# Scaling the low words of float64 weights on GpSimd instead of ScalarE in an attention and gating kernel

## The chip, the cores and the metric

The kernel runs on one core of a Trainium2 chip. The core has five engines with queues of their own: TensorE (PE, matrix products and transposes into PSUM), VectorE (DVE), ScalarE (ACT), GpSimd (POOL) and SyncE (SP, which here issues most of the DMA transfers). Each takes its own queue in order, and an instruction starts when its engine has come to it and the semaphores it waits for are set. The metric is the device time of one execution in microseconds (us), as the median of several runs. PEld is the loading of weights into PE, which overlaps the products.

## The reference

Attention with a bias from running sums, then two gated mixing layers. B = 4 batches, H = 8 heads, S = 576 positions, D = 64.

```python
scores = scale * np.matmul(q, k.transpose(0, 1, 3, 2))
cum = np.cumsum(np.maximum(s, 0.0), axis=-1)
bias = -(cum[:, :, :, None] - cum[:, :, None, :])
scores = np.where(causal, -1000000000.0, scores + np.minimum(bias, 0.0))
attn = np.exp(scores - np.max(scores, axis=-1, keepdims=True))
attn = attn / (np.sum(attn, axis=-1, keepdims=True) + 1e-09)
x = np.matmul(attn, v)                    # heads side by side: (B, S, 512)
...
gate = 1.0 / (1.0 + np.exp(-gate_pre))    # gate_pre: 5-tap causal convolution of x with conv_w
x = gate * (x @ w_val) @ w_out
...
h = np.maximum(x @ w_in, 0.0)
u, v = h[..., :512], h[..., 512:]
v_n = (v - mean(v)) / np.sqrt(var(v) + 1e-06)
v_s = np.einsum('ts,bsd->btd', w_spatial, v_n) + b_spatial[None, :, None]
out = (u * v_s) @ w_out
```

The inputs q, k, v and s arrive as float32. The scale factors that build the dense weights are float64 numbers, so the weights w_val, conv_w, w_out (of both layers) and w_in arrive as float64, and the kernel turns them into float32 itself, then splits each into a high and a low part for products of more than one pass.

## The kernel before

The program runs over 32 heads (8 per batch). For one head, `scores` lets PE form score tiles in PSUM (L222, from head 8 on L224 and L225), DVE adds the mask and takes the row's extreme (L233, tiles p and nm), and ACT takes the exponential (L238). `transposes` turns p on PE (L279) and ACT copies the result to pt (L281). After every second head, `pv` multiplies by v (L303) and DVE scales with the reciprocal sums R into x (L306 to L309). R takes a way of its own: DVE forms the reciprocals rin (L248), PE transposes them (psr, L253), ACT copies them (rt, L255) and issues a store to r_d (L256), and SP loads them back, spread over the partitions (R, L262). `conv` then forms z from x on ACT (L318) and DVE (L321).

Between the heads, `more` draws background work from a queue of Python generators. For the first 16 heads this is the preparation of the weights. `first_steps` starts with conv_w, then prepares w_out and w_val chunk by chunk, then the first half of w_in, and folds w_out into w_in on PE (`fold`, L420 to L422). `second_steps` and `third_steps` do the rest, beside the first batch's mixing (`mixing_a`, `mixing_b`). From the second batch on, the mixing of a batch runs between the heads of the next one. The sigmoid of z runs on ACT (L514, for the last batch L517); between exponentials and sigmoids ACT loads another function table.

Each chunk of float64 weights goes through `from_f64`. SP loads 128 x 512 pairs of 32-bit words into r (tile wg for the early chunks with k below 3, else wr). `up` and `low` are every second word of r. ACT takes the absolute value of the upper words (L382, into a), DVE clamps it (L383), masks the sign (L384) and shifts and joins (L385); ACT scales the lower words by 2^-29 with a rounding to int32 (L388), and POOL adds both parts as integers (L389). Then `fold_prep` or `weight_prep` takes the high part on ACT (L73, `hi_of`) and the low part on DVE (L80, `lo_of`). There are 21 such conversions, 20 of full size and the small one of conv_w. The first 13 are held behind the last score reading on DVE (`paced`). POOL has little else to do: the low parts of gated values (g and y) and of v, and two small steps of the normalisation (L557, L559).

The order in each engine's queue is not the order of the code. The program is built with a scheduler that simulates the queues and puts the instructions of all engines into an order by priority and its own estimates of durations.

Of the kernel before, what the change touches and what calls it, by code (L numbers as in the profile page):

```python
# [10 lines left out]
U32 = mybir.dt.uint32  # L11
AF = mybir.ActivationFunctionType
ALU = mybir.AluOpType
# [11 lines left out]
def tile_stickbreak_attention_moe(  # L25
# [39 lines left out]
    V, G, A, T, SY = nc.vector, nc.gpsimd, nc.scalar, nc.tensor, nc.sync  # L65

    def f(ap):
        return ap.bitcast(F32)
# [65 lines left out]
    def tmp(name, dt=F32):  # L134
        return mid.tile([128, S], dt, tag="tmp", name=name, bufs=2)
# [230 lines left out]
    def from_f64(src, n):  # L366

        k = count[0] % 5
        count[0] += 1
        if count[0] <= 13 and k < 3:  # L370
            if k == 0 and "g" not in W:
                W["g"] = mid.tile([128, NP * (2 * S + 64)], I32, tag="g", name="wg")
            r = W["g"][:, k * 1536:k * 1536 + 1024]
            a = f(W["g"][:, k * 1536 + 1024:k * 1536 + 1536])
        else:
            r = mid.tile([128, 1024], I32, tag="wr", name="wr", bufs=2)
            a = tmp("wa")
        W["r"] = r
        r, a = r.rearrange("p (c t) -> p c t", t=2)[:, 0:n, :], a[:, 0:n]
        SY.dma_start(r, src.rearrange("p (c t) -> p c t", t=2))  # L380
        up, low = r[:, :, 1], r[:, :, 0]
        A.activation(a, f(up), AF.Abs, scale=65536.0)  # L382
        V.tensor_scalar(out=a, in0=a, scalar1=F64_HIGH, scalar2=F64_LOW, op0=ALU.min, op1=ALU.max)  # L383
        V.tensor_scalar(out=up, in0=up, scalar1=-2 ** 31, scalar2=None, op0=ALU.bitwise_and)  # L384
        V.scalar_tensor_tensor(out=up, in0=a.bitcast(I32), scalar=3, in1=up, op0=ALU.logical_shift_left,  # L385
                               op1=ALU.bitwise_or)

        A.activation(low, low.bitcast(U32), AF.Copy, scale=2.0 ** -29)  # L388
        G.tensor_tensor(out=a.bitcast(I32), in0=low, in1=up, op=ALU.add)  # L389
        return a  # L390

    @paced
    def fold_prep(kc, j):

        if j is None:
            wh, wl, src = wo_h, wo_l, woT[:, kc * 1024:(kc + 1) * 1024]
        else:
            if j not in wi:
                wi[j] = [wtmp.tile([128, NP, 512], F32R, tag=f"wi{x}", name=f"wi{x}") for x in "hl"]
            wh, wl = wi[j]  # L400
            src = w_in[:, kc, j * 1024:(j + 1) * 1024]
        t = from_f64(src, 512)
        hi_of(A, wh[:, kc, :], t)
        lo_of(V, wl[:, kc, :], t, wh[:, kc, :])

    @paced
    def weight_prep(src, dst, mc):
        t = from_f64(src[mc], 512)
        w = W["r"].rearrange("p (t c) -> p t c", t=2).bitcast(F32R)
        hi_of(A, w[:, 0, :], t)  # L410
        lo_of(V, w[:, 1, :], t, w[:, 0, :])
        SY.dma_start(dst[mc], f(w))
# [218 lines left out]
    def first_steps():  # L631
        nonlocal cw
        cw = early.tile([128, NP, 5], F32, name="cw")
        V.tensor_copy(cw, from_f64(conv_w, 20).rearrange("p (c k) -> p c k", k=5))
        order = [(lambda mc=mc: weight_prep(w_val, wv_d, mc)) for mc in KC]
        order += [(lambda mc=mc: fold_prep(mc, None)) for mc in KC]
        order = order[4:] + order[:4]
        for o in order:
            o()
            yield  # L640
        for kc in KC:
            fold_prep(kc, 1)
            yield
        for ec in range(4):
            fold(ec, 1)
            yield 2.56
# [140 lines left out]
```

## Time and profile before

| | us |
|---|---|
| median of 3 runs | 516.34 (516.25 to 516.61) |
| the profiled execution | 515.71 |
| its span | 513.9 |
| PE, DVE, ACT, POOL busy | 481.8, 315.6, 338.5, 128.3 |
| mean granted clock of PE | 0.987 |

The rows come from one profiled execution. A row names the source line, the engine, the operation, the tiles written and read (numbers of buffers left out), the shape, and then durations; "<-" behind an idle time names what ended it. Times of a stretch are counted from the span's start.

### The profile page before, as it was taken

The page shows a single profiled execution, that of the slowest core. Times are in us where ns is not written, and L with a number is a line of the kernel's source. Part 1 is how long each engine was busy: PE and PEld are TensorE (multiplying, and loading weights), DVE is VectorE, ACT ScalarE, POOL GpSimd, SP SyncE. Part 2 cuts the span into 40 slices and gives each one's busy share as a digit, 9 for nine tenths or more (in the row PEclk, how much of TensorE's full clock was granted, in tenths as well). Part 3 has the DMA queues.
Part 4 walks back from the last instruction along what each step waited for, and adds up shares of the span by engine and source line. Part 5 has one row for each costly group of instructions (what it writes and reads, how often), then busy time and mean ns, then how long its engine had stood idle before and what let it go on. Part 6 is the DMA issues. An engine that isn't in the chain of part 4 may idle for free.

```text
span 513.9 us, 9133 instructions
## 1 busy us (share of the span) xinstructions
PE 481.8 (94%) x3138; PEld 402.4 (78%) x3138; DVE 315.6 (61%) x835; ACT 338.5 (66%) x819; POOL 128.3 (25%) x162
## 2 busy tenths in 40 slices
PE   8697978879999999998999999899998999999997
PEld 5454545767778887986969897888878889998997
DVE  5588988878978984843579476544767435125120
ACT  2999797697787965893748666785889724225322
POOL 5121112017360104101235023002243013146140
PEclk9798989999999999999999999999999999999999
DMA  3964897346752644276640413675611071700002
GB/s 92 253 206 145 263 331 191 110 112 214 238 197 82 185 145 124 74 215 198 179 119 13 131 39 87 186 221 169 177 28 34 5 248 45 237 2 1 0 8 86
DMA packets 51855, 69.28 MB, mean 135 GB/s; under 512 B 23968, under 2 KB 39488, under 8 KB 51808
## 3 DMA queue, kind: packets, MB, share of 16 engines
q1 hardware_dynamic: 46880, 63.88, 42.2%
q10 hardware_dynamic: 4928, 4.80, 2.8%
q8 instruction: 25, 0.41, 0.3%
q14 instruction: 22, 0.18, 0.1%
HBM read 55.96 MB, written 9.16 MB: 127 GB/s over the span
## 4 chain that ended last, share of the span: by engine, by line
PE 49%; ACT 3%; DMA 3%; issue 1%; DVE 1%; ACTq 0%; DVEq 0%
PE psm L420 9%; PE psm L421 9%; PE psm L422 9%; PE pso L303 5%; PE pst L279 4%; PE psm L592 3%; PE psm L594 2%; PE psm L593 2%; PE pss L224 2%; DMA out<-ot 2%; PE pss L225 2%; DMA wv<-wv_d 1%; ACT L238 1%; PE psm L595 1%; PE psm L596 1%
## 5 line engine op out<-in xcount | busy, mean ns | idle before, releaser
L238 ACT ACTIVATE p<-p,nm 64x64 f32<-64x64 f32 (+4 forms) x160 | 88.4, 554 | 10.7 <-DVE nm L233 10.3
L281 ACT ACTIVATE pt<-pst 128x512 f32<-128x512 f32 (+2 forms) x128 | 60.2, 498 | 30.0 <-PE pst L279 24.3
L233 DVE CUSTOM_DVE_ANT_0 p<-pss,mask 64x64 f32<-64x64 f32 (+4 forms) x160 | 63.0, 413 | 19.3 <-PE pss L225 8.5
L279 PE MATMUL pst<-ident,p 128*128 128x128 f32 x416 | 64.3, 281 | 3.2 <-ACT p L238 3.2
L80 POOL TENSOR_TENSOR g<-gt,g 128x288 fp32r<-128x288 f32 x32 | 29.3, 918 | 125.5 <-ACT g L73 100.1
L279 PEld LDWEIGHTS pst<-ident,p 128*128 128x128 f32 x416 | 51.2, 145 | 10.9 <-ACT p L238 4.5
L321 DVE SCALAR_TENSOR_TENSOR z<-x,cw,z 128x575 f32<-128x575 f32 (+1 forms) x64 | 55.2, 863 | 7.1 <-ACT z L318 6.6
L80 POOL TENSOR_TENSOR y<-gt,y 128x288 fp32r<-128x288 f32 x32 | 27.8, 872 | 111.2 <-ACT y L73 111.2
L303 PE MATMUL pso<-pt,vraw 128*64 128x512 f32 (+4 forms) x320 | 54.0, 446 | 0.1
L224 PE MATMUL pss<-qk 128*64 128x64 f32 (+1 forms) x144 | 43.6, 321 | 1.8 <-ACT pt L281 1.2
L225 PE MATMUL pss<-kd,cn 66*64 66x64 f32 (+1 forms) x144 | 41.4, 295 | 0.0
L222 PE MATMUL pss<-raw 128*128 128x320 f32 (+4 forms) x96 | 32.2, 448 | 8.6 <-DVE nm L233 5.3
L420 PE MATMUL psm<-g,wch 128*128 128x288 f32 x128 | 38.4, 304 | 1.3 <-ACT v L544 1.3
L497 DVE TENSOR_TENSOR gt<-psm,z 128x288 f32<-128x288 f32 x32 | 14.5, 454 | 40.7 <-PE psm L422 33.0
L303 PEld LDWEIGHTS pso<-pt,vraw 128*64 128x64 f32 (+1 forms) x320 | 19.5, 137 | 25.3 <-issue 17.6
L592 PE MATMUL psm<-wsh,vh 128*128 128x288 f32 x128 | 38.3, 303 | 0.4 <-DVE gt L497 0.4
L593 PE MATMUL psm<-wsh,vl 128*128 128x288 f32 x128 | 37.6, 298 | 0.0
L422 PE MATMUL psm<-g,wch 128*128 128x288 f32 x128 | 37.5, 297 | 0.0
L594 PE MATMUL psm<-wsl,vh 128*128 128x288 f32 x128 | 37.5, 296 | 0.0
L421 PE MATMUL psm<-g,wcl 128*128 128x288 f32 x128 | 37.4, 295 | 0.0
L497 DVE TENSOR_TENSOR gt<-psm,u 128x288 f32<-128x288 f32 x32 | 14.5, 454 | 35.1 <-PE psm L596 26.5
L420 PE MATMUL psm<-y,wv 128*128 128x288 f32 x96 | 29.2, 305 | 3.8 <-ACT ot L607 3.7
(168 smaller groups left out, 1327.0 us busy)
## 6 DMA issues: line engine op xcount, KB each, us to landing
raw<-in_qk SPq DMA_DIRECT2D x24, 448.0 KB
wv<-wv_d SPq DMA_DIRECT2D x12, 512.0 KB
wv<-wo_d SPq DMA_DIRECT2D x12, 512.0 KB
R<-r_d SPq DMA_DIRECT2D x32, 160.0 KB
out<-ot ACTq DMA_DIRECT2D x32, 144.0 KB
vraw<-in_vp SPq DMA_DIRECT2D x32, 128.0 KB
cn<-qk SPq DMA_DIRECT2D x24, 144.0 KB
raw<-in_qk SPq DMA_DIRECT2D x48, 64.0 KB
```

What stands on the lines that cost most here:

```text
L80: eng.tensor_tensor(out=out_, in0=in_, in1=f(hi), op=ALU.subtract)
L224: T.matmul(pst[0:m, o:o + b - a], qa[:, q0:q0 + m], kb[:, k0 + a:k0 + b], start=True, stop=False)
L233: LAST["V"] = V.tensor_tensor_reduce(out=row[:, a:b], in0=src, in1=mask[0:m, o:o + b - a], scale=-0.125, scalar=3.0e38 if a == 0 else nm[0 ...
L238: A.activation(row, row, AF.Exp, bias=nm[0:m, i:i + 1], scale=-1.0, accum_out=sm[h // 2 % 2][0:m, h % 2, i:i + 1])
L279: T.transpose(pt[:, 128 * t:128 * t + 128], p[:, o:o + 128], ident[:, way:way + 128])
L281: A.activation(PT[h][:, to:to + n], pt[:, o:o + n], AF.Copy)
L303: m = T.matmul(to[64 * j:64 * j + 64], vs[j][k0:, 4 + (c == 4) if c > 3 else c, :], pts[j][k0:, o:o + to.shape[1]], start=c in (0, 5), sto ...
L321: V.scalar_tensor_tensor(out=z[:, d:], in0=x[:, :S - d], scalar=cw[:, p, k:k + 1], in1=z[:, d:], op0=ALU.mult, op1=ALU.add)
L420: T.matmul(pt, ah, bh, start=j == 0, stop=False)
L421: T.matmul(pt, al, bh, start=False, stop=False)
L422: T.matmul(pt, ah, bl, start=False, stop=j == n - 1)
L592: T.matmul(o, vh[c][:, cs], wsh[:, c, hs[hf]], start=c == 0, stop=False)
```

## The change

One line of `from_f64` changes. The scaling of the lower words, with the rounding to int32, is issued to POOL as a multiplication by a scalar instead of to ACT as a copy with a scale. The add that follows was on POOL before and stays there.

```diff
@@ -385,7 +385,7 @@
         V.scalar_tensor_tensor(out=up, in0=a.bitcast(I32), scalar=3, in1=up, op0=ALU.logical_shift_left,
                                op1=ALU.bitwise_or)
 
-        A.activation(low, low.bitcast(U32), AF.Copy, scale=2.0 ** -29)
+        G.tensor_scalar(out=low, in0=low.bitcast(U32), scalar1=2.0 ** -29, scalar2=None, op0=ALU.mult)
         G.tensor_tensor(out=a.bitcast(I32), in0=low, in1=up, op=ALU.add)
         return a
```

Since the scheduler lays out all queues anew, the order differs on every engine from the second head on. Each engine has the same instructions as before, but for the 21 that move from ACT to POOL and two more table loads on ACT.

The first place is POOL's queue during the conversions of w_out (in the early heads); wg_183 is the shared tile of the early chunks, wr and wa with a number are the words and the result of one later chunk, and + marks what is new at this place.

```order
+L388 TENSOR_SCALAR wr_260<-wr_260 128x512
+L389 TENSOR_TENSOR wg_183<-wg_183 128x512
+L388 TENSOR_SCALAR wr_322<-wr_322 128x512
+L389 TENSOR_TENSOR wa_261<-wr_260 128x512
+L388 TENSOR_SCALAR wg_183<-wg_183 128x512 x2
+L389 TENSOR_TENSOR wa_323<-wr_322 128x512
```

Where adds (L389) stood one behind the other before, the scaling of the next chunk now stands between them, ahead of the add of the chunk before it.

The second place is DVE's queue around x1, the x of the second pair of heads. nm_744 belongs to head 7 and nm_575 to head 5; the rows without an input read out a sum. Before:

```order
L233 ISA p1_128,nm_744<-pss_762,mask_99 128x320
L233 ISA nm_744 128x1
L385 SCALAR_TENSOR_TENSOR wg_183<-wg_183 128x512
L233 ISA p1_128,nm_744<-pss_788,mask_99 128x448
L233 ISA nm_744 128x1
L306 TENSOR_TENSOR x1_552<-pso_553,R_523 128x384
L308 TENSOR_TENSOR x1_552<-pso_553,R_523 128x128
L309 TENSOR_TENSOR x1_552<-psq_554,R_523 128x64
L80 TENSOR_TENSOR wil_604<-wa_606,wih_603 128x512
```

and in the changed kernel:

```order
L233 ISA p1_128,nm_575<-pss_593,mask_99 128x320
L233 ISA nm_575 128x1
L383 TENSOR_SCALAR wa_606<-wa_606 128x512
L384 TENSOR_SCALAR wr_605<-wr_605 128x512
L306 TENSOR_TENSOR x1_552<-pso_553,R_523 128x384
L308 TENSOR_TENSOR x1_552<-pso_553,R_523 128x128
L309 TENSOR_TENSOR x1_552<-psq_554,R_523 128x64
L233 ISA p1_128,nm_575<-pss_616,mask_99 128x448
```

x1 has moved up by two heads. Its reciprocal, rin_468, stood 53 rows ahead of it and now stands 26 rows ahead. On PE, the products of the same pair (L303) stood behind the first score tiles of head 6 and now stand ahead of those of head 5.

The third place is ACT's queue at the last head: z_4084 is the gate of the last batch, L580 a copy of the mixing. Before:

```order
L238 ACTIVATE p1_128,sm1_122<-p1_128,nm_4699 128x576
L580 ACTIVATE u_4610<-psm_4769 128x288
L281 ACTIVATE pt_4709<-pst_4738 128x512
L281 ACTIVATE pt_4709<-pst_4763 128x512
L580 ACTIVATE u_4610<-psm_4796 128x288
L517 ACT_TABLE_LOAD
L517 ACTIVATE z_4084<-z_4084 128x576
```

and in the changed kernel:

```order
L580 ACTIVATE u_4610<-psm_4744 128x288
L517 ACT_TABLE_LOAD
L517 ACTIVATE z_4084<-z_4084 128x576
L238 ACT_TABLE_LOAD
L238 ACTIVATE p1_128,sm1_122<-p1_128,nm_4699 128x576
L580 ACTIVATE u_4610<-psm_4769 128x288
L580 ACTIVATE u_4610<-psm_4796 128x288
```

The third sigmoid of the last batch has moved ahead of the last exponential, which takes one more table load here, and one more before the fourth sigmoid.

## Rows read from the trace of the kernel before

**Rows 1.** The page: busy time, share and instructions by engine; granted clock in 40 slices.

```profile
PE 481.8 (94%) x3138; PEld 402.4 (78%) x3138; DVE 315.6 (61%) x835; ACT 338.5 (66%) x819; POOL 128.3 (25%) x162
...
PEclk9798989999999999999999999999999999999999
```

**Rows 2.** Busy time by stretch: length, then PE, PEld, DVE, ACT, POOL; clock, DMA.

```profile
10.00:28.00 18.00, 13.90 (x56) 9.20 (x55) 10.12 (x44) 14.18 (x42) 2.29 (x3) 0.81 0.90 252
28.00:82.00 54.00, 46.03 (x240) 27.58 (x239) 49.05 (x129) 47.76 (x120) 12.10 (x10) 0.94 0.74 228
82.00:110.00 28.00, 21.50 (x124) 15.76 (x122) 22.92 (x63) 21.28 (x44) 1.27 (x1) 1.00 0.43 109
110.00:190.00 80.00, 79.63 (x514) 65.98 (x515) 67.13 (x161) 63.27 (x158) 27.49 (x29) 1.00 0.59 184
190.00:513.90 323.90, 312.49 (x2188) 277.89 (x2186) 160.26 (x424) 189.51 (x454) 78.09 (x98) 1.00 0.36 104
```

**Rows 3.** Waits in 28 to 82 us (R: 10 to 110): total, times, longest.

```profile
PE pss L222 <- DVE nm L233: 5.3, 9, 1.4
PE psr L253 <- DVE x L309: 1.4, 1, 1.4
PE pss L224 <- ACT pt L281: 1.2, 1, 1.2
...
DVE p L233 <- PE pst L279: 2.2, 3, 1.3
DVE p L233 <- PE pss L222: 1.3, 3, 0.8
...
ACT wr L73 <- POOL wa L389: 2.2, 1, 2.2
...
DVE x L306 <- DMA R<-r_d: 4.5, 3, 1.6
```

**Rows 4.** L388 in 28 to 82 us (ns min/median/max); two ACT rows, in order of time.

```profile
L388 ACT ACTIVATE wg<-wg x6: 662/680/706, 32.2 to 72.3; 128x512 int32<-128x512 uint32 x6
L388 ACT ACTIVATE wr<-wr x5: 662/694/717, 29.8 to 79.1; 128x512 int32<-128x512 uint32 x5
...
16.26 0.68 ACT L388 ACTIVATE wg<-wg 128x512 int32<-128x512 uint32 x1
16.82 0.45 ACT L238 ACTIVATE p<-p,nm 128x192 f32<-128x192 f32 x1
```

**Rows 5.** In order of time: start us, us; then line L384 on DVE.

```profile
34.59 1.10 POOL L389 TENSOR_TENSOR wa<-wr 128x512 int32<-128x512 int32 x1 [2.87 <-ACT wo_h L73]
34.71 1.27 DVE L384 TENSOR_SCALAR wg<-wg 128x512 int32<-128x512 int32 x1
...
79.76 1.48 DVE L80 TENSOR_TENSOR kd<-raw,qk 64x576 fp32r<-64x576 f32 x1
...
L384 DVE TENSOR_SCALAR wg<-wg x9: 169/415/1274, 13.6 to 77.3; 128x512 int32<-128x512 int32 x8, 128x20 int32<-128x20 int32 x1
```

**Rows 6.** POOL operations by line: ns min/median/max, first and last start.

```profile
L104 POOL TENSOR_SCALAR_AFFINE_SELECT ident<-ident x2: 241/268/295, 6.2 to 6.4; 128x128 f32<-128x128 f32 x1, 128x64 f32<-128x64 f32 x1
...
L389 POOL TENSOR_TENSOR wa<-wr x12: 1038/1072/1367, 30.4 to 174.4; 128x512 int32<-128x512 int32 x12
...
L80 POOL TENSOR_TENSOR vl<-v,vh x16: 1277/1296/1721, 141.2 to 473.6; 128x512 fp32r<-128x512 f32 x16
```

**Rows 7.** In order of time: the way of R for the second pair.

```profile
45.61 0.20 DVE L248 RECIPROCAL rin<-den 128x10 f32<-128x10 f32 x1
52.36 0.28 ACTq L256 DMA_DIRECT2D r_d<-rt  x1
59.16 1.30 SPq L262 DMA_DIRECT2D R<-r_d  x2
66.76 0.56 DVE L306 TENSOR_TENSOR x<-pso,R 128x384 f32<-128x384 f32 x1 [1.50 <-DMA R<-r_d]
```

**Rows 8.** Groups by line: the table loads of the last batch's sigmoids.

```profile
L517 ACT ACT_TABLE_LOAD x3 | 3.8, 1283 | 0.1
```

## The prediction

> **What bounds the kernel now.** I read the page first [rows 1]: TensorE (PE) is busy 481.8 us of a span of 513.9 us, so all the slack that any change can find is some 32 us. The clock line shows that the granted clock dips in the second, fourth and sixth of forty slices and is nearly full afterwards. Then the table by stretches [rows 2] says which stretch can move. From 110 to 190 us PE is busy 79.63 of 80.00 us, and from 190 us on 312.49 of 323.90: there PE alone sets the pace, and VectorE (DVE), ScalarE (ACT) and GpSimd (POOL) wait for it. The slack lies before 110 us, in the first eight heads, into which the kernel packs the conversion of the float64 weights. In 28 to 82 us three engines are nearly full at once: DVE 49.05 of 54 us, ACT 47.76, PE 46.03 at a clock of 0.94. Of the 21 conversions, 11 have their scaling step (L388 on ACT) in this stretch [rows 4]. So this stretch decides, and the question is whether ACT or DVE sets its pace.
>
> The waits answer it [rows 3]. In these 54 us PE waits 5.3 us for DVE's reading of the scores (L233, nine times) and 1.4 us for DVE's x; it waits for ACT 1.2 us, once. DVE itself waits 2.2 us for the transposes on PE and 1.3 us for score tiles on PE, and 1.5 us for the transfer R (at 66.76 us) [rows 7]; ACT waits 2.2 us for POOL, once. DVE is the engine that the others wait for most. ACT is as full, but rarely awaited.
>
> **What is removed.** 21 ACT instructions, of which 20 handle 128x512. One is listed with 0.68 us, but the next one on ACT starts 0.56 us after it (16.26 to 16.82 us) [rows 4], so it costs ACT's queue 0.56 us. In 28 to 82 us that is 11 x 0.56 = 6.2 us less on ACT, over the whole kernel 20 x 0.56 = 11.2 us. In 10 to 28 us ACT is busy 14.18 of 18, and from 82 to 110 us 21.28 of 28 [rows 2]: with idle time there already I count nothing. After 110 us PE hides it.
>
> What can the 6.2 us buy? PE waits for ACT only 1.2 us directly. DVE's 2.2 us behind the transposes are ACT's too, since those transposes read what ACT's exponential writes. If both go, DVE still idles 1.3 + 1.5 = 2.8 us. So the stretch can fall to DVE's own work plus 2.8 us, which with DVE as it is would be 49.05 + 2.8 = 51.85 us: **a gain of at most 2.15 us**, not 6.2.
>
> **What is added.** 21 POOL instructions on the same tiles. No row shows a one-input POOL operation of 512 columns. From below: AFFINE_SELECT, one input, takes 0.295 us for 128 columns and 0.241 us for 64 [rows 6], 0.84 ns a column, so 0.295 + 384 x 0.00084 = 0.62 us for 512. From above: the two-input integer add of the same tile, median 1.07 us, and the fp32r subtraction that writes vl, 1.30 us [rows 6]. Having one input it is nearest to the lower row; I take 0.7 us, a little more, since it also converts twice and steps over every second word.
>
> POOL has room: 12.1 us busy of 54 [rows 2], plus 11 x 0.7 = 7.7. But POOL's work is not free to DVE. The order of time shows it [rows 5]: the add on POOL starts at 34.59 us and lasts 1.10 us, and the DVE operation that starts at 34.71 lasts 1.27 us, where the median of its line is 0.42 us. DVE stood still until POOL ended. This happens seven times in the stretch, at 34.71 (first), 37.83, 42.34, 54.73, 59.80, 70.98 and 79.76 us (last), with 0.85 + 0.55 + 0.84 + 0.79 + 0.37 + 0.85 + 0.79 = 5.04 us over the normal durations. For the 10 POOL operations of the stretch [rows 2] that is **0.50 us of DVE for each**, at some 1.04 us of POOL.
>
> For 0.7 us it is 0.50 x 0.7 / 1.04 = 0.34 us each, and 11 x 0.34 = 3.7 us on DVE. The bounds: nothing, if POOL always waits its turn instead; 11 x 0.50 = 5.5 us at 1.04 us of POOL; 6.8 us at 1.30 us. Sum for the stretch: 49.05 + 3.7 + 2.8 = 55.55 us against 54, **+1.55 us**; by the bounds -2.15 to +4.65 us.
>
> A page of the Trainium skill speaks against the change: "SBUF — State Buffer", section "SBUF: two separate sides", says that DVE and GpSimd share a port pair as "an exclusive lock, not a bandwidth split", held for the whole instruction by whoever starts first. The trace agrees with it [rows 5]. Taken strictly, each POOL operation can cost DVE its full 0.7 us, and the sum would be 49.05 + 7.7 + 2.8 = 59.55 us, +5.55 us; the rows' mean, where three of ten meet nothing, stays my price.
>
> **What is moved.** The program's order is written by a scheduler, and because one operation changed engine it differs on all queues from the second head on. Three places matter.
>
> POOL's queue (first order piece): the scaling of a chunk now stands ahead of the add of the chunk before it. It needs only its load; if that is late, the add behind it waits, and with it ACT's rounding copy, which waits for POOL already (2.2 us) [rows 3]. I count nothing, since the load is what ACT's Abs (L382) of the same chunk needs too, and no wait for it is among ACT's in the stretch; if the cover is gone, another 2.2 us.
>
> DVE's queue (second piece): x of the second pair of heads stood among the scores of head 7 and now stands among those of head 5, 26 rows behind its reciprocal instead of 53. Before, reciprocal to x took 45.61 to 66.76 us and still ended in 1.5 us of waiting for R [rows 7]. Nothing in the forecast; a rival below.
>
> ACT's tail (third piece): two more table loads, because exponentials and sigmoids alternate once more at the end. At 1.283 us each [rows 8] that is 2.6 us of ACT. ACT has 189.5 us of work in the last 324 [rows 2], so I count nothing; uncovered, 2.6 us.
>
> From 110 us on, the remaining POOL operations add 6 x 0.34 = 2 us to DVE's 67 of 80 us, behind a full PE: 0. PE idles 11.4 us after 190 us, and the new order can deal these waits anew; I allow 2 us both ways in the range.
>
> **Sum.** +1.55 us on the profiled execution, 515.71 us (span 513.9), gives 517.26 us. That execution lies 0.63 us below the median of the runs, 516.34; for the median the forecast is 516.34 + 1.55 = **517.9 us**.
>
> **The rivals.**
>
> *ACT sets the pace after all (faster).* ACT has 47.76 us of the 54 and loses 6.2. Its exponentials and copies feed the transposes in PE's queue, and in the new order PE has the products of the second pair (L303) ahead of head 5's scores, where they stood among head 6's: work for the time in which PE now waits for DVE. PE is idle 54 - 46.03 = 8.0 us in the stretch; filling half of it gives 516.34 - 4 = 512.3 us. Against it: 6.7 of PE's 7.9 us of waits there name DVE, and DVE gets more work. It decides if the port costs DVE clearly under 2.15 / 11 = 0.20 us per operation.
>
> *The two cancel (same).* 11 x 0.20 = 2.2 us on DVE against 2.15 us gained: 516.3 us.
>
> *DVE stands at x (slower still).* With half the rows between reciprocal and x, 21.15 x 26 / 53 = 10.4 us, the chain of transposed sums, ACT copy, store and load R may not fit: it took 6.75 us to the store's issue at 52.36 us, and R, issued at 59.16, was there 7.6 us later [rows 7]. A stay of 2.5 us at each of three x in the first eight heads, less the 4.5 us paid already [rows 3], is +3 us on top of the forecast: 520.9 us. For it: DVE takes its queue in order, so the next head's scores stand behind x. Against it: the chain's own steps move forward too.
>
> *The change does not do what it says.* All 21 operations stand on POOL in the new order and none on ACT, so this has no chance worth naming.
>
> **How the numbers follow.** Forecast 0.33, x rival 0.12, faster 0.33, same 0.22. A difference of 0.2% (1.03 us) is about what a measurement of this kernel can tell from no change: faster is below 515.3, slower above 517.4. Slower thus has 0.33 + 0.12 = 0.45, same 0.22, faster 0.33. The forecast's own range, by its bounds above no change, is 516.3 to 521.0. The range for 8 in 10 reaches into the faster case: 512.5 to 521.0, with about a tenth left out at each end.
>
> **What would show it.** In the profile after: L388 on POOL between 0.62 and 1.07 us; DVE operations on SBUF data stretched beside it, with DVE busy above 51 us in a stretch that answers to 28 to 82; ACT some 6 us less busy there; PE's waits in it still naming L233. The forecast is wrong if PE's idle time before 110 us shrinks while DVE's busy time hardly grows, if L388 on POOL takes far more than 1.3 us, or if the time moves after 190 us, where I count nothing. Waits of x for R above 4.5 us before 110 us would point to the x rival.

## The result

The changed kernel takes 521.6 us in the median of seven executions, where the kernel before took 516.3 us in as many: a ratio of 1.0068, 95% interval 1.004 to 1.0096. A second timing gave 521.6 us against 516.8, a ratio of 1.0089 (1.0067 to 1.011). So the change costs 3.5 us (0.68% of 516.3) to 5.3 us (the difference of the first two medians). The forecast had the sign and 1.55 us. One trace of those below (pool_old_order) fell in a disturbed execution, and of it I use the first 176 us alone.

The profiled execution of the changed kernel has a span of 517.9 us. First its page, the lines that answer to [rows 1] (engine: busy us, share, instructions; below them the granted clock in forty slices):

```profile
PE 486.1 (94%) x3138; PEld 404.2 (78%) x3138; DVE 325.2 (63%) x835; ACT 330.2 (64%) x800; POOL 160.0 (31%) x183
...
PEclk9999798999999999999999999999998999999999
```

POOL's busy time went from 128.3 to 160.0 us and DVE's from 315.6 to 325.2; ACT's fell from 338.5 to 330.2. Then the table by stretches, which answers to [rows 2] (length, then PE, PEld, DVE, ACT, POOL; granted clock, DMA share, GB/s):

```profile
10.00:28.00 18.00, 12.49 (x61) 7.63 (x59) 12.75 (x44) 13.78 (x42) 8.90 (x8) 1.00 0.85 247
28.00:82.00 54.00, 44.83 (x222) 26.37 (x223) 50.66 (x130) 41.15 (x105) 30.43 (x22) 0.93 0.74 229
82.00:110.00 28.00, 26.21 (x161) 20.51 (x160) 25.58 (x73) 22.91 (x55) 2.22 (x1) 0.96 0.51 140
110.00:190.00 80.00, 77.42 (x497) 64.16 (x496) 69.60 (x155) 59.01 (x148) 35.95 (x34) 1.00 0.57 173
190.00:517.90 327.90, 317.01 (x2180) 279.70 (x2178) 160.36 (x418) 190.72 (x450) 75.44 (x98) 0.99 0.35 103
```

A stretch is cut by time, so the two kernels have partly different work in it. Between 28 and 82 us ACT is 6.6 us less busy (47.76 before, 41.15 now), POOL 18.3 us more, DVE 1.6 us more. From 110 to 190 us PE, which was busy 79.63 of 80 us, now idles 2.6 us. The scaling itself, to be set beside [rows 4] (ns: shortest, median, longest; first and last start):

```profile
L388 POOL TENSOR_SCALAR wr<-wr x12: 1576/1658/2220, 22.3 to 150.6; 128x512 int32<-128x512 uint32 x12
L388 POOL TENSOR_SCALAR wg<-wg x9: 301/1594/2128, 13.3 to 68.4; 128x512 int32<-128x512 uint32 x8, 128x20 int32<-128x20 uint32 x1
```

One takes 1.6 us, not 0.7. And the waits in 28 to 82 us, to be set beside [rows 3] (total, times, longest):

```profile
PE pss L222 <- DVE nm L233: 7.1, 9, 1.4
...
DVE wil L80 <- ACT wih L73: 3.1, 1, 3.1
...
PE psm L422 <- DVE wil L80: 2.1, 1, 2.1
```

PE's waits for DVE's reading of the scores rose from 5.3 to 7.1 us, and a new one of 2.1 us stands for the lower words wil. No wait of x for the transfer R is left: 4.5 us of it stood in [rows 3].

### The profile page after: what moved, and what is told of

It is laid out like the page before. It is cut to its first block, busy times and chain, and to the rows that moved or that the text cites. A ratio compares the mean times of both kernels' runs of the same rounds, so it can differ in the third digit from the quotient of the medians.

```text
span 517.9 us, 9141 instructions
## 1 busy us (share of the span) xinstructions
PE 486.1 (94%) x3138; PEld 404.2 (78%) x3138; DVE 325.2 (63%) x835; ACT 330.2 (64%) x800; POOL 160.0 (31%) x183
## 4 chain that ended last, share of the span: by engine, by line
PE 63%; DVE 19%; ACT 8%; DMA 5%; issue 3%; SPq 1%; POOL 0%; DVEq 0%; ACTq 0%; POOLq 0%
PE psm L420 12%; PE psm L421 11%; PE psm L422 11%; PE pso L303 7%; PE pst L279 5%; DVE p L233 3%; DVE z L321 3%; PE psm L592 3%; PE psm L593 3%; PE psm L594 3%; PE pss L224 2%; DMA raw<-in_qk 2%; PE pss L225 2%; DVE kd L80 2%; ACT p L238 1%
## 5 line engine op out<-in xcount | busy, mean ns | idle before, releaser
L233 DVE CUSTOM_DVE_ANT_0 p<-pss,mask 64x64 f32<-64x64 f32 (+4 forms) x160 | 62.3, 411 | 20.5 <-PE pss L225 14.7
L80 POOL TENSOR_TENSOR g<-gt,g 128x288 fp32r<-128x288 f32 x32 | 28.2, 885 | 125.5 <-ACT g L73 122.3
L321 DVE SCALAR_TENSOR_TENSOR z<-x,cw,z 128x575 f32<-128x575 f32 (+3 forms) x64 | 53.4, 840 | 6.9 <-ACT z L318 6.3
L303 PE MATMUL pso<-pt,vraw 128*64 128x512 f32 (+4 forms) x320 | 55.9, 437 | 0.7 <-ACT pt L281 0.7
L222 PE MATMUL pss<-raw 128*128 128x320 f32 (+4 forms) x96 | 32.3, 439 | 10.9 <-DVE nm L233 7.8
L420 PE MATMUL psm<-g,wch 128*128 128x288 f32 x128 | 38.8, 306 | 0.0
L303 PEld LDWEIGHTS pso<-pt,vraw 128*64 128x64 f32 (+1 forms) x320 | 19.7, 135 | 23.8 <-issue 14.6
L422 PE MATMUL psm<-g,wch 128*128 128x288 f32 x128 | 38.2, 302 | 0.0
L73 ACT ACTIVATE qk<-raw 128x576 fp32r<-128x576 f32 x48 | 30.2, 678 | 4.8 <-PE pss L224 4.8
```

The source lines that it names most:

```text
L80: eng.tensor_tensor(out=out_, in0=in_, in1=f(hi), op=ALU.subtract)
L233: LAST["V"] = V.tensor_tensor_reduce(out=row[:, a:b], in0=src, in1=mask[0:m, o:o + b - a], scale=-0.125, scalar=3.0e38 if a == 0 else nm[0 ...
L303: m = T.matmul(to[64 * j:64 * j + 64], vs[j][k0:, 4 + (c == 4) if c > 3 else c, :], pts[j][k0:, o:o + to.shape[1]], start=c in (0, 5), sto ...
L321: V.scalar_tensor_tensor(out=z[:, d:], in0=x[:, :S - d], scalar=cw[:, p, k:k + 1], in1=z[:, d:], op0=ALU.mult, op1=ALU.add)
L420: T.matmul(pt, ah, bh, start=j == 0, stop=False)
L422: T.matmul(pt, ah, bl, start=False, stop=j == n - 1)
```

## The experiments

The change does two things at once: it moves an operation to another engine, and the scheduler then writes another order for all queues. To part them, most kernels below hold every queue in a given order. The kernel is written as before, and at its end each instruction is tied to the one ahead of it on its engine, by issue order alone and with no wait:

```python
def hold(tc, nc):
    traced = {i.name: i for i in nc.cur_bb.bb.instructions}
    info = mybir.DependencyInfo(mybir.DependencyClass.NoSync, mybir.DependencyReason.DATA)
    for rows in json.loads(zlib.decompress(base64.b64decode(ORDER))):
        for a, b in zip(rows, rows[1:]):
            tc.add_manual_dep(traced[f"I-{b}"], f"I-{a}", info, reason="order")
```

ORDER is the list of instruction numbers per engine, read from the built program of the kernel before ("old order") or of the changed kernel ("new order"). Two kernels in one order have the same instructions in the same places on PE, DVE and SP, so that their traces can be laid on each other instruction by instruction.

For that I use a landmark: the start of PE's transposition of the sums (L253), which runs once for each pair of heads. The fifth one lies near 116 us in the old order and 102 us in the new one, the seventh near 173 and 167 us. These are the rows (start, us) of the kernel before, of pool_old_again, of act_new_order and of the changed kernel, in this order, the fifth and the seventh of each:

```profile
116.20 0.27 PE L253 MATMUL psr<-ident,rin 128*10 128x128 f32 x1
173.23 0.27 PE L253 MATMUL psr<-ident,rin 128*10 128x128 f32 x1
...
117.69 0.27 PE L253 MATMUL psr<-ident,rin 128*10 128x128 f32 x1
176.94 0.27 PE L253 MATMUL psr<-ident,rin 128*10 128x128 f32 x1
...
102.15 0.27 PE L253 MATMUL psr<-ident,rin 128*10 128x128 f32 x1
167.43 0.28 PE L253 MATMUL psr<-ident,rin 128*10 128x128 f32 x1
...
103.92 0.27 PE L253 MATMUL psr<-ident,rin 128*10 128x128 f32 x1
170.05 0.28 PE L253 MATMUL psr<-ident,rin 128*10 128x128 f32 x1
```

All traces and times together (ratio to the kernel before, timed beside it, with its 95% interval; then the two landmarks and the way between them, us):

| run | order | scaling | ratio | fifth | seventh | between |
|---|---|---|---|---|---|---|
| the kernel before | old | ACT | | 116.20 | 173.23 | 57.03 |
| before_again | old | ACT | 1.0013 (0.999 to 1.0037) | 115.96 | 173.01 | 57.05 |
| pool_forms | old | ACT | not timed | 114.72 | 171.75 | 57.03 |
| no_scaling16 | old | none to the 16th chunk | 1.0047 (1.0011 to 1.0083) | 115.85 | 173.19 | 57.34 |
| extra_pool14 | old | ACT, and 14 operations more on POOL | 1.0015 (0.999 to 1.0041) | 114.26 | 171.53 | 57.27 |
| pool_old_order | old | POOL | 1.0057 (1.0027 to 1.0086) | 117.76 | 175.75 | 57.99 |
| pool_old_again | old | POOL | 1.0038 (1.0006 to 1.007) | 117.69 | 176.94 | 59.25 |
| act_new_order | new | ACT | 1.0011 (0.9989 to 1.0033) | 102.15 | 167.43 | 65.28 |
| mixed_order | new, then old | ACT | 0.9926 (0.9897 to 0.9955) | 101.26 | 165.56 | 64.30 |
| no_scaling_new16 | new | none to the 16th chunk | 0.9987 (0.9952 to 1.0021) | 102.34 | 166.90 | 64.56 |
| extra_new15 | new | ACT, and 15 operations more on POOL | 1.0029 (1.0001 to 1.0057) | 105.01 | 169.28 | 64.27 |
| the changed kernel | new | POOL | 1.0068 (1.004 to 1.0096) | 103.92 | 170.05 | 66.13 |
| after_again | new | POOL | 1.0089 (1.0067 to 1.011) | 103.91 | 169.85 | 65.94 |
| pool_mixed | new, then old | POOL | 0.9989 (0.9965 to 1.0014) | 105.77 | 171.81 | 66.04 |

Equal programs differ by up to 1.5 us at the fifth landmark (the first three rows), and by 0.02 us on the way between the two. But other pairs that are alike so far differ more: pool_old_order and pool_old_again, one program, by 1.3 us on the way between; act_new_order and mixed_order, which have one order up to 290 us, by 1.0 us there; the changed kernel and pool_mixed, also alike up to 290 us, by 1.9 us at the fifth landmark. Part of the spread at the fifth landmark may be the clock. Before it, the traces have this much time at a granted clock of 0.5, the lower of its two levels (1.2 and 2.4 GHz): in the old order 13.7 us (no_scaling16 17.1); in the new one mixed_order 6.8, act_new_order, no_scaling_new16, extra_new15 and the changed kernel 10.2, after_again 13.7, pool_mixed 17.1. Between the two landmarks no trace has any. So a difference under some 2 us at the fifth landmark, or 1 us between the two, says little by itself.

**Controls.** The kernel before against itself, and the changed kernel once more. No edit.

> The kernel before, unchanged, timed against itself. Both theories: a ratio of 1.000, within 0.002. It serves to see the granted clock of several executions of the kernel before, of which only one is known (0.987), and the spread between equal programs.

> The changed kernel, unchanged, on the same chip as the two variants of this call. Both theories: a ratio of 1.004 to 1.010 again, some 519 to 522 us.

Both came as expected. An equal program differs by 0.13%, inside its interval, so a variant's ratio under about 1.003 says little by itself.

**The operation or the order.** One variant has the change's line and the old order, with each scaling right ahead of its own add on POOL; the other has the line of before and the new order.

```diff
 # pool_old_order: the changed kernel
         tile_stickbreak_attention_moe(tc, *args, o)
+        hold(tc, nc)    # ORDER: of the kernel before, L388 ahead of its L389 on POOL
 # act_new_order: the kernel before
         tile_stickbreak_attention_moe(tc, *args, o)
+        hold(tc, nc)    # ORDER: of the changed kernel, L388 behind its L382 on ACT
```

> The scaling on GpSimd (L388), but every other instruction of all five queues is held in the order of the kernel before; each scaling stands right ahead of its own add. Theory ENGINE (the loss comes from the operation itself: GpSimd's 1.6 us in place of the 0.7 forecast, which hold up VectorE before 110 us): the time stays that of the changed kernel, 519 to 522 us, ratio 1.005 to 1.010. Theory ORDER (the loss comes from the scheduler's new order, above all after 190 us, where TensorE waits for exponentials behind the added table load): within 1.5 us of the kernel before, 515 to 518 us, ratio 0.998 to 1.003.

> The scaling stays on ScalarE, right behind the Abs of its chunk, but every other instruction of all five queues is held in the order of the changed kernel. Theory ENGINE: the time of the kernel before, 515 to 518 us, ratio 0.998 to 1.003. Theory ORDER: the time of the changed kernel, 519 to 522 us, ratio 1.005 to 1.010. If both of these variants lie between, each theory has its share.

The operation costs, in either order: pool_old_order is at 1.0057, and in the new order, where act_new_order with the scaling on ACT is at 1.0011, the operation is worth 1.0089 / 1.0011, 0.8% or 4.0 us. In the new order a lower clock comes with it: the mean granted clock is 0.988 over act_new_order's twelve executions and 0.981 over after_again's six (in the old order it is 0.981 for before_again and pool_old_order alike). At 0.984 after_again takes 520.3 us against 519.0 for act_new_order, at 0.987 521.2 against 517.4; so 1.3 to 3.7 us are left at equal clock, from few executions, and how much of the 4.0 us the clock has is open. That the order alone costs nothing (0.1%) holds for the sum; it will turn out that it gains early and loses late.

**What ACT's relief is worth.** The scaling of the first 16 chunks is left out and their add takes zeros; all else stands in the old order (EXTRA collects added instructions, which ORDER places).

```diff
+    zero = mid.tile([128, 512], F32, tag="v", name="zero", bufs=3).bitcast(I32)
+    EXTRA.append(G.memset(zero, 0))
...
-        A.activation(low, low.bitcast(U32), AF.Copy, scale=2.0 ** -29)
-        G.tensor_tensor(out=a.bitcast(I32), in0=low, in1=up, op=ALU.add)
+        count[0] <= 16 or A.activation(low, low.bitcast(U32), AF.Copy, scale=2.0 ** -29)
+        G.tensor_tensor(out=a.bitcast(I32), in0=zero[:, 0:n] if count[0] <= 16 else low, in1=up, op=ALU.add)
```

> The order of the kernel before on all queues, but the scaling (L388) is left out of the first 16 chunks altogether, on ScalarE and on GpSimd: the add takes a tile of zeros in its place, so that the low words are dropped from these weights. It shows what ScalarE's relief alone is worth. Theory BALANCE (ScalarE's relief gains what the prediction gave it, and VectorE's stretching takes more than that): TensorE is 1.5 to 2.5 us ahead of the kernel before at 110 us, and the time is 513.5 to 515.5 us. Theory RELIEF IS NOTHING (VectorE alone sets the pace before 110 us): within 0.5 us at 110 us, ratio 0.998 to 1.002.

Nothing that shows, as the second theory had it. The stretch from 28 to 82 us has 6.9 us less on ACT than [rows 2]:

```profile
28.00:82.00 54.00, 43.67 (x218) 26.51 (x219) 49.33 (x123) 40.84 (x106) 14.91 (x10) 0.91 0.76 233
```

but the fifth landmark stands at 115.85 us, within those of the kernel before (114.72 to 116.20), and the time is not better (1.0047). Its trace has 3.4 us more at the lower clock before that landmark, behind which up to 1.7 us of relief could hide (an estimate: half of 3.4); the time of twelve executions shows no gain either. That it is worse by its interval, with less work in the kernel, I can't explain; the landmark says that it isn't lost before 173 us. It also means that a ratio of this size in the old order is no proof by itself that an operation costs.

**What POOL's work costs DVE.** The scaling stays on ACT, and POOL runs as many operations of its kind on a scratch tile.

```diff
+    extra = mid.tile([128, 512], F32, tag="v", name="extra", bufs=3).bitcast(I32); EXTRA.append(G.memset(extra, 0))
+    EXTRA.extend(G.tensor_scalar(out=extra, in0=extra.bitcast(U32), scalar1=2.0 ** -29, scalar2=None, op0=ALU.mult) for _ in range(14))
...
```

> The order of the kernel before on all queues, the scaling stays on ScalarE, and GpSimd runs 14 more operations of the scaling's kind (128x512, int32 from uint32, contiguous) on a scratch tile that nobody waits for, each right ahead of an add, where the scaling stands in the variant with the old order. It shows GpSimd's price alone, without ScalarE's relief. Theory BALANCE: TensorE is 3 to 4.5 us behind the kernel before at 110 us (the 1.6 us of the variant and the relief that is not had here), VectorE is 4 to 5 us busier by then, time 519 to 522 us. Theory RELIEF IS NOTHING: 1 to 2 us behind at 110 us, 517.5 to 519.5 us. A theory CHAIN (what costs is that each chunk's add comes later because the scaling is slower on GpSimd): 0 to 0.5 us behind, 516 to 518 us, since no add waits for the scratch operations.

The operations are as long as the scaling on POOL (ns: shortest, median, longest):

```profile
L353 POOL TENSOR_SCALAR extra<-extra x14: 1489/1550/2083, 14.9 to 110.8; 128x512 int32<-128x512 uint32 x14
```

and DVE's instructions up to 112 us, each against its twin in the kernel before, last 4.0 us longer in sum. No cost shows: the fifth landmark is at 114.26 us, the earliest of the old order, and the ratio is 1.0015 (0.999 to 1.0041). So the theory that I had forecast by, that ACT's relief gains and DVE's stretching takes more, is borne out in the old order in neither half. Where the 4.0 us went, DVE's own waits show. Of DVE in 10 to 110 us, first in before_again, then here (total, times, longest):

```profile
DVE x L306 <- DMA R<-r_d: 5.8, 4, 1.5
DVE p L233 <- PE pss L222: 4.8, 7, 2.5
...
DVE p L233 <- PE pss L222: 3.6, 6, 1.9
DVE x L306 <- DMA R<-r_d: 3.5, 4, 1.7
```

DVE waits 3.5 us less for R and for the scores (2.7 to 4.4 us, by which of the three traces of the kernel before is taken): it had the time. Of the theories named, these two runs leave CHAIN for the old order. The second trace with the scaling on POOL in that order:

> The variant pool_old_order once more, for a second trace and twelve more times, since its one trace fell in a disturbed execution. Theory VECTOR alone (as extra_pool14 and no_scaling16 have it, nothing is lost in the old order): within 0.5 us of the kernel before at 110 us, ratio 0.999 to 1.003. If the waits of ScalarE for the adds (2 us more in its trace) are real: 1.5 to 2 us behind at 110 us again, ratio 1.004 to 1.008.

It repeats the loss: 117.69 us at the fifth landmark, 2.1 us behind the mean of the three traces of before (115.6). At the seventh landmark both traces with the scaling on POOL are 2.5 us or more behind the other five of the old order. What CHAIN says is that the adds come later for those who need them. ACT's waits for adds in 10 to 156 us, before_again first, then pool_old_again:

```profile
ACT wr L73 <- POOL wa L389: 3.0, 2, 2.6
ACT wih L73 <- POOL wg L389: 0.6, 1, 0.6
...
ACT wr L73 <- POOL wa L389: 3.9, 3, 2.6
ACT wih L73 <- POOL wa L389: 1.5, 1, 1.5
```

They are 1.8 us longer, at an engine whose queue goes in order. But no_scaling16 has 4.7 us of such waits, 1.1 us more than before_again, and is not late. So that they are the loss of 2.1 us in the old order is argued, not shown, and its cause stays open there: no run took away these waits alone.

**The same in the new order.**

> The changed kernel's order on all queues, the scaling on ScalarE (as in act_new_order), and 15 more GpSimd operations of the scaling's kind on a scratch tile, at the places where the scaling stands on GpSimd in the changed kernel. In the old order such extra work cost nothing. Theory VECTOR (in the new order VectorE sets the pace, and what GpSimd takes from it is paid): VectorE 4 to 6 us busier by 110 us, TensorE 2 to 3 us behind act_new_order at 150 us, 2 to 5 us more waiting of TensorE for the reading of scores (L233), time 519.5 to 522 us. Theory QUEUE (the loss is the adds that come later because a scaling stands ahead of them and waits for its load): within 1 us of act_new_order at 150 us, 516.5 to 518.5 us.

> The changed kernel's order on all queues, the scaling left out of the first 16 chunks (the add takes zeros, the low words of these weights are dropped). ScalarE's relief alone, in the new order. Theory VECTOR: worth little, 0 to 1 us ahead of act_new_order at 150 us, 516 to 518 us. Theory ACT (ScalarE sets the pace in the new order): 2 us or more ahead, 514 to 516 us.

Here the extra work on POOL shows at the fifth landmark: 105.01 us in its one trace, 3.3 us behind the mean of the two traces with the scaling on ACT (101.7), and 2.9 us behind act_new_order, which has as much time at the lower clock before it. The three with the scaling on POOL are 2.8 us behind (104.5), the changed kernel, again with as much time at the lower clock, 1.8 us behind act_new_order. DVE's instructions last 4.3 us longer by then, those of the changed kernel 5.4 us (4.2 and 4.9 in pool_mixed and after_again). PE's waits for the reading of the scores (L222 for L233) in 10 to 110 us are 1.1 and 2.7 us with the scaling on ACT, 4.3 with the extra work, 5.7 to 7.8 with the scaling on POOL; but no_scaling_new16 has 5.4 us of them and is not late. DVE has less in reserve here: in 10 to 110 us its x waits 2.5 us for R in act_new_order and not at all in mixed_order and the changed kernel, where it was 4.5 us in the kernel before.

By the time the cost of the extra work is not clear of the noise: 1.0029 against 1.0011 for act_new_order, with intervals that overlap, where the scaling on POOL has 1.0068 and 1.0089. Its 519.58 us lies in the range that VECTOR named, but on a chip where the kernel before takes 518.7. So that VECTOR holds in the new order rests on one landmark. ACT's relief again shows no gain: 102.34 us at the fifth landmark, with as much time at the lower clock as act_new_order (102.15), and a ratio of 0.9987 whose interval overlaps with that of 1.0011.

A part of what the extra work lacks against the scaling is the way between the landmarks. There, extra_new15 has 64.27 us, like the kernels with the scaling on ACT (64.30 and 65.28), since its extra work ends before it; with the scaling on POOL it is 65.94 to 66.13 us, 0.7 to 1.9 us longer, and 1.0 to 2.2 us longer in the old order (57.99 and 59.25 against 57.0). Five scalings lie there, in a stretch where PE was thought full. The changed kernel's waits in 112 to 182 us, of PE, and one of DVE in 112 to 156 us:

```profile
PE psm L420 <- DVE gt L497: 1.0, 1, 1.0
PE psr L253 <- DVE rin L248: 0.9, 1, 0.9
PE psm L420 <- DVE v L550: 0.7, 1, 0.7
...
DVE v L561 <- POOL rs L559: 1.4, 3, 0.7
```

Of these PE waits act_new_order has 1.0, 0.5 and 0.3 us, extra_new15 the first alone and mixed_order none; DVE's wait for rs is 0.2 us in these three and 1.4 to 1.7 with the scaling on POOL. POOL has 25.3 us of work between 112 and 156 us in the kernel before, products of the gate and parts of the normalisation, for which DVE waits in its turn. That five times 1.6 us more on that queue come out at PE is argued from these waits, not shown by a run of its own.

**What the operation costs by itself.** 18 operations behind all of POOL's own work, three of each form.

```diff
+    extra = mid.tile([128, 1024], I32, tag="wr", name="extra", bufs=2)
+    low, flat = extra.rearrange("p (c t) -> p c t", t=2)[:, :, 0], extra[:, 0:512]
+    for out_, in_ in ((low, low.bitcast(U32)), (flat, flat.bitcast(U32)), (f(low), f(low)), (f(flat), f(flat)),
+                      (f(flat), flat.bitcast(U32)), (flat, f(flat))):
+        EXTRA.extend(G.tensor_scalar(out=out_, in0=in_, scalar1=2.0 ** -29, scalar2=None, op0=ALU.mult) for _ in range(3))
```

> The kernel before in its own order, with 18 more GpSimd operations of 128x512 on a scratch tile at the end of GpSimd's queue, after 475 us, three each of: int32 from uint32 with every second word (the scaling's own form), int32 from uint32 contiguous, float from float with every second word, float from float contiguous, float from uint32 contiguous, int32 from float contiguous. If the conversion from integers costs, the second takes about 1.6 us like the first and the fourth 0.62 to 0.7; if the stride costs, the first and the third take 1.6 and the others 0.7; if a multiplication on GpSimd costs that whatever the type, all six take 1.6 us. The time itself: 515 to 519 us unless GpSimd's tail outlasts the rest.

The third case. By shape (busy us, mean ns; each row joins every second word and contiguous):

```profile
L742 POOL TENSOR_SCALAR extra<-extra 128x512 int32<-128x512 uint32 x6 | 9.1, 1525 | 0.5
L742 POOL TENSOR_SCALAR extra<-extra 128x512 f32<-128x512 f32 x6 | 9.1, 1509 | 0.5
L742 POOL TENSOR_SCALAR extra<-extra 128x512 f32<-128x512 uint32 x3 | 4.5, 1487 | 0.2
L742 POOL TENSOR_SCALAR extra<-extra 128x512 int32<-128x512 f32 x3 | 4.5, 1487 | 0.2
```

A multiplication by a constant over 512 columns takes POOL 1.49 us with nothing beside it (the shortest to longest of all 18: 1.49 to 1.57), whatever the type and the stride. The tail outlasts the rest, so the time of 531.3 us is that of the 18.

**The best order.** The new order up to the eleventh pair's x, the old one from there.

```diff
         tile_stickbreak_attention_moe(tc, *args, o)
+        hold(tc, nc)    # ORDER: of the changed kernel up to the eleventh pair's L309, then what is left as in the kernel before
```

> The scaling on ScalarE as in the kernel before; all queues in the new order (with the scaling on ScalarE) up to the product with R of the eleventh pair of heads, near 290 us, and what is left in the order of the kernel before, with its twelve table loads. Theory ORDER HAS TWO HALVES (the new order gains 2 to 4 us before 200 us and loses 4 to 6 after 310 us): 512 to 515 us, ratio 0.990 to 0.997. If the early gain is only work that is taken ahead and given back: 516 to 518 us, ratio 0.998 to 1.002.

> The change in the best order found (mixed_order, 512.7 us with the scaling on ScalarE): the scaling on GpSimd, all else held as there. If the operation itself costs 2 to 4 us whatever the order, 515 to 517 us, TensorE 2 to 4 us behind mixed_order at 150 us. If the loss hangs on the order alone, 512 to 513.5 us.

With the scaling on ACT this is faster than both kernels: 512.7 us against 517.0 for the kernel before on the same chip, 0.9926 (0.9897 to 0.9955). With the scaling on POOL the gain is lost again, 0.9989, and the landmarks are 4.5 and 6.3 us behind mixed_order (with 10.2 us more at the lower clock before the fifth): the operation costs here too. So the new order has two halves. The first gains some 0.7%; the second, which mixed_order leaves out, gives it back, since act_new_order is at 1.0011. From the first of PE's products at which the two orders part, the stretch to the end is this, in the changed kernel and in mixed_order (length, then PE, PEld, DVE, ACT, POOL; granted clock, DMA share, GB/s):

```profile
290.50:517.90 227.40, 219.20 (x1501) 195.99 (x1499) 98.89 (x252) 122.80 (x285) 51.51 (x68) 0.99 0.29 88
287.80:510.40 222.60, 214.50 (x1501) 194.83 (x1499) 98.42 (x253) 121.84 (x284) 53.76 (x68) 0.99 0.31 90
```

It is 4.8 us longer in the changed kernel, and PE does not idle more in it (8.2 and 8.1 us): it is busy 4.7 us longer with the same products. Of these, 3.2 us stand at one place, the products of the twelfth pair with v (L303, 24 of them). In the new order each two of them stand between background products; in the old one 16 come in one go. First the busy time of L303 around that pair and its first rows in the changed kernel, then in mixed_order:

```profile
314.00:326.00 12.00, 7.89 (x24) 2.28 (x24) 1.00 0.30 74
314.30 1.07 PE L303 MATMUL pso<-pt,vraw 128*64 128x512 f32 x2
315.31 0.40 PE L420 MATMUL psm<-y,wv 128*128 128x288 f32 x1
...
311.00:323.00 12.00, 4.72 (x24) 1.73 (x24) 1.00 0.57 145
312.17 2.20 PE L303 MATMUL pso<-pt,vraw 128*64 128x512 f32 x16
```

All five traces with the new order's second half have 7.89 us there, and mixed_order, pool_mixed and the kernel before 4.71 or 4.72. That the alternation is the reason is argued: no run changed it alone. What the other 1.5 us are I did not part further.

Two things that look like causes are not what tells the halves apart. One batch's last sigmoid and exponential alternate once more in the changed kernel, and PE waits 1.20 us for the exponential behind the added table load; but behind 290 us the waits of PE are as long in sum in mixed_order (4.8 us against 4.9), mostly for other results of ACT.

```profile
410.65 1.28 ACT L238 ACT_TABLE_LOAD   x1
...
412.87 0.76 PE L279 MATMUL pst<-ident,p 128*128 128x128 f32 x5 [1.20 <-ACT p L238]
```

And PE's granted clock falls in 380 to 400 us of the changed kernel, behind a wait of PE of 1.7 us for an exponential, which ended at 389.7 us; in mixed_order it falls near 333 us:

```profile
380.00:400.00 20.00, 18.30 (x107) 15.12 (x105) 13.89 (x39) 18.03 (x42) 6.50 (x10) 0.91 0.10 28
...
331.00:336.00 5.00, 5.00 (x27) 4.91 (x26) 2.92 (x8) 3.77 (x12) 0.00 (x0) 0.66 0.73 211
```

A granted clock of 0.91 over 20 us is the lower level for 3.6 us of them (20 x 0.09 / 0.5), and 0.66 over 5 us is the lower level for 3.4 us: as much in either half. The stretch near 390 us stands in four of the five traces with the new order's second half, and in neither of mixed_order and pool_mixed, which have theirs near 333 and 340 us.

## Why the prediction was right, and where it was not

The direction was right. By the ratio the time is 1.0068 x 516.34 = 519.9 us, inside the range of 512.5 to 521.0; the plain median, 521.6, lies just above it. The size, 1.55 us, was less than half of what was measured, and the way there was right in part only. That the sign came out is in part luck: the gain was counted too high, the operation's length less than half of what it is, and its hold on DVE for each us too strong. By its steps:

- **Which stretch decides.** Right in part: in the new order the scaling on POOL loses 2.8 us by the fifth landmark, 1.8 us between the two traces of equal clock. Wrong for what follows: I counted the six operations from 110 us on at nothing, "behind a full PE". PE was full there (79.63 of 80 us, [rows 2]) but 0.7 to 2.2 us went, most likely because DVE and POOL, which feed it, had little in hand. A full engine hides work on others only as long as they stay ahead of it.
- **What is removed.** The 6.2 us less on ACT came (6.6 us). The bound of 2.15 us that this could buy was too high: in either order no gain showed. The waits pointed that way, since PE waited for ACT only 1.2 us ([rows 3]); I should not have added the 2.2 us behind the transposes as ACT's.
- **The length of the scaling on POOL.** The worst-sized term: 0.7 us forecast, 1.6 measured, and even alone 1.49. I went by AFFINE_SELECT because it has one input too, and the number of inputs turned out to be no guide: the two-input add takes 1.07 us in the median over the same columns [rows 6]. Even the upper bound, 1.30 us for vl, was too low.
- **What it costs DVE.** 0.34 us for each operation was forecast; in the changed kernel DVE's instructions up to 110 us last 5.4 us longer for 16 scalings, 0.34 us each (0.26 and 0.31 in pool_mixed and after_again). The number is near by two errors that cancel: the operation is 2.3 times as long, and it holds DVE up less for each us than an add does. POOL and DVE of the changed kernel, in order of time, and at the end the usual length of L385 in the kernel before:

```profile
15.66 1.59 POOL L388 TENSOR_SCALAR wg<-wg 128x512 int32<-128x512 uint32 x1 [1.34 <-DMA wg<-in_woT]
16.62 0.92 DVE L383 TENSOR_SCALAR wg<-wg 128x512 f32<-128x512 f32 x1
...
70.65 1.64 POOL L388 TENSOR_SCALAR wr<-wr 128x512 int32<-128x512 uint32 x1 [0.69 <-DMA wr<-in_w_in]
72.37 1.16 POOL L389 TENSOR_TENSOR wg<-wg 128x512 int32<-128x512 int32 x1
...
71.17 0.72 DVE L385 SCALAR_TENSOR_TENSOR wg<-wg 128x512 int32<-128x512 int32 x1
...
72.56 1.26 DVE L384 TENSOR_SCALAR wg<-wg 128x512 int32<-128x512 int32 x1
...
L385 DVE SCALAR_TENSOR_TENSOR wg<-wg x9: 180/683/694, 13.8 to 78.3; 128x512 int32<-128x512 int32 x8, 128x20 int32<-128x20 int32 x1
```

  Beside the scaling, DVE's L385, which reads two inputs, takes 0.72 us, near its usual 0.68; others are held up, by half a us at most (L383 at 16.62 us takes 0.92 where 0.42 is usual). Beside the add, L384 stands until the add ends (0.42 us usually [rows 5], 1.26 here). Against act_new_order, 1.2 of the 5.4 us are of instructions that meet nothing but the scaling and 5.0 of instructions that an add meets; those that meet neither are 0.8 us shorter. The rule of the Trainium skill, "SBUF — State Buffer", section "SBUF: two separate sides", that the port pair which DVE and GpSimd share is locked for the whole instruction, against a DVE operation with two SBUF inputs too, agrees here with the two-input add and not with the scaling.
- **DVE sets the pace.** Not so in the old order, where 4.0 us on DVE cost nothing that shows; in the new one extra work on POOL alone is 2.9 to 3.3 us late at the fifth landmark of one trace, but by the time only 0.9 us slower, inside the noise. I read it from a profile in the old order. That DVE is awaited most did not mean that it had no time to spare: it waited 4.5 us for R itself [rows 3].
- **What is moved.** POOL's queue was counted at nothing "since the load is what ACT's Abs needs too"; the scaling in front of other work is, as argued above, what costs between the landmarks and perhaps in the old order. x for R, which was a rival for more, went the other way: its waits for R vanished. The two table loads were counted at nothing; PE waits 1.2 us for one of them, but no longer in sum behind 290 us than in mixed_order. No term of the forecast has what the new order loses there, 3.2 us of it at the twelfth pair's products. The allowance of 2 us for the new order's later waits was too small in each half (0.7% gained, 0.9% lost), and good only for their sum.
- **The rivals.** ACT setting the pace is not borne out by the two runs without the scaling. That both cancel falls by the interval. The strict lock's +5.55 us for the stretch, worked out with 0.7 us for the scaling, is more than was measured, though the scaling is more than twice as long.
- **The signs.** ACT's 6 us less and PE's waits for L233 came; DVE above 51 us in the stretch did not quite (50.66). Two of the signs of being wrong came too: L388 takes 1.6 us, above the 1.3 named though not far above, and the stretch behind 190 us grew from 323.90 to 327.90 us.

## What to carry to other kernels

Taking work from a busy engine gains only if it is the one that others wait for; leaving the work out altogether in one run shows the most that moving it can gain, and here no gain showed. Where a scheduler writes the order, hold one order and change the operation, then hold the operation and change the order: here the operation cost some 4 us in the new order, and that order gained about as much in one half and lost it in the other, so that its better half with the other order's tail is the fastest kernel of this study. Before a wait or a dip of the clock is called the cause of such a loss, look whether the faster kernel has one as long elsewhere. An operation moved to a quiet engine is priced by an operation of its own kind, and by the queue that it joins.

## What was not expected of the hardware

- POOL's multiplication by a constant takes 1.49 us over 128x512, longer than its two-input integer add of the same columns (1.07 us in the median), for integers and floating-point numbers, contiguous or every second word.
- DVE beside such an operation is held up by half a us at most (0.92 where 0.42 is usual) and at times hardly (0.72 where 0.68 is usual), though it is stopped by POOL's two-input add until that ends (1.26 where 0.42 is usual); the scaling itself grows from 1.49 us by itself to as much as 2.22 in the changed kernel.
- The 24 products of one pair with v keep PE busy for 7.89 us where each two stand between other products, and for 4.72 us where 16 come in one go.
- The same wait of PE for an exponential, 1.7 us near 388 us, is followed by the lower clock in four of five traces of the same order, and in the fifth it is not.
